# Three-step preparation of w_in's chunks, another order of the first loads, and 768 columns as two halves of 384

## Chip, cores and metric

The kernel runs on one core of one Trainium2 chip. The metric is the device time of one execution in microseconds; the kernel before takes 1076.66 us (median of three runs, 1076.47 to 1077.52).

## What is computed

Sigmoid attention over 4 batches of 12 heads (448 tokens, head width 64), then a gated block with a spatial mixing, then a residual two-layer block. The reference, cut:

```python
scores = scale * q @ k.T - log(S);  attn = sigmoid(scores);  x = attn @ v      # x: 4 x 448 x 768
h = relu(x @ w_in); u, v = h[..., :512], h[..., 512:]                          # w_in: 768 x 1024
v_n = (v - mean(v)) / sqrt(var(v) + 1e-6)
v_s = einsum('ts,bsd->btd', w_spatial, v_n) + b_spatial
x = (u * v_s) @ w_out                                                          # 512 x 768
xn = (x - mean(x)) / sqrt(var(x) + 1e-6) * g_ln
out = x + relu(xn @ w_ch1) @ w_ch2                                             # 768 x 3072 x 768
```

## The kernel before

**Products.** Every float32 operand of the large products is kept as a high and a low part; `mm3` (lines 252 to 255) issues three TensorE products for one: high x high, high x low, low x high. The instructions run in the order in which the code issues them; nothing reorders them. Each engine works through its own queue in order, and SyncE issues nearly all DMAs in order.

**w_in.** Its eight chunks of 768 columns (four of `wv_chunks`, then four of `wu_chunks`) arrive as raw 64-bit numbers. `w_load` (line 262) fetches one into one of two raw buffers. `w_decode` (267 to 283) makes a float32 of it: a scale on GpSimd for these chunks (line 273; ScalarE, line 275, for the chunks of the other weights), then three bit operations on VectorE (276, 277, 280). `split` (285) copies the high part on ScalarE (286) and subtracts on VectorE (287). `weight_jobs` (306) lines the steps up as load i, decode i-1, split i-2, and `jobs.pop` takes them from that line; the list `EARLY` says how many at each `beside()`. The first load stands ahead of the loop (line 775), before the first v load and the q and k loads of pair 2.

**Attention.** The loop of line 796 takes two head pairs an iteration, 12 iterations in all. An iteration issues: `rests` (line 415 products, one sigmoid, line 429 products, `x_end` of the pair before last), scores of two blocks (line 402), `sums` (line 442) and `x_end` of the last pair, the q and k loads of later pairs and `beside`, two more blocks, `sums`, `qk_split` of the next pairs (VectorE casts 381 and 384, GpSimd subtractions 385 and 386), two more blocks, `qk_split`, and then `bg.run`, the filler: the products of `x @ w_in` for batches already finished (`hv` with 512 columns, `hu` with 448), up to 9.2 us of them by the code's own costs. `hv` goes on with a block of w_in when its chunks were split at least `LAG` steps ago; `hu` starts when all eight were. Scores and rests write the tile `ps` with two buffers, sums the tile `psa` with two buffers, which `x_end` (line 286 copy, line 287 subtraction) frees.

**Wide outputs.** 768 output columns are written into the two PSUM banks of one `ps2` tile as 512 and 256 columns (`SPLIT`, `wide`). That happens in `Project.step`, 14 tiles with 24 products each, and in `ch2` of the last block, 12 groups of 14 tiles with 12 products each (lines 699 to 709); line 695 adds a tile to the residual. The very last tile is made as two parts, each added and stored by itself.

Of the kernel before, what the change touches and what calls it, by code (L numbers as in the profile page):

```python
# [10 lines left out]
F32 = mybir.dt.float32  # L11
# [3 lines left out]
ALU = mybir.AluOpType  # L15
# [12 lines left out]
NT = B * S  # L28
NCH = NT // P
HALF = DM // 2  # L30
SPLIT = [(0, 512), (512, 256)]
NB2 = 2 * S // P
EPS = 1e-6

# [5 lines left out]

BG_US = 2.3

LAG = 2
WARM = 10


EARLY = [1, 0, 0, 2, 0, 2, 1, 2, 1, 2, 1, 2, 1, 2, 1, 2]
WO_FROM = 30

VN_DVE = [range(4), range(4), (1, 3), (1, 3)]  # L50
# [153 lines left out]
def sigmoid_attention_gmlp_mlp(ctx: ExitStack, tc, q, k, v, w_in, w_sp, w_out, g_ln, w1, w2, out):  # L204
# [37 lines left out]
    def ps1():  # L242
        singles.append(singles.pop(0))
        return singles[-1]()

    def ps2():
        return ps_s.tile([P, 2, 512], F32, tag="ps2", name="ps2")

    def wide():
        return ps2().rearrange("p a n -> p (a n)")[:, :DM]  # L250

    def mm3(ps, lh, ll, rh, rl, first, last):
        nc.tensor.matmul(ps, lh, rh, start=first, stop=False)  # L253
        nc.tensor.matmul(ps, lh, rl, start=False, stop=False)  # L254
        nc.tensor.matmul(ps, ll, rh, start=False, stop=last)  # L255
# [8 lines left out]
        nc.sync.dma_start(raw.rearrange("p n t -> p (n t)"), src.bitcast(U32))  # L264
        return raw

    def w_decode(raw, first):
        blk = dec_r.next()
        f, bits = blk.ap(WC), blk.bits(WC)
        low, high = raw[:, :, 0], raw[:, :, 1]  # L270

        if first:
            nc.gpsimd.tensor_scalar(f, high.bitcast(F32), 2.0**-112, None, op0=ALU.mult)  # L273
        else:
            nc.scalar.mul(f, high.bitcast(F32), 2.0**-112)
        nc.vector.tensor_scalar(bits, bits, 3, None, op0=ALU.logical_shift_left)
        nc.vector.scalar_tensor_tensor(  # L277
            bits, low, 29, bits, op0=ALU.logical_shift_right, op1=ALU.bitwise_or
        )
        nc.vector.scalar_tensor_tensor(  # L280
            bits, high, 0x80000000, bits, op0=ALU.bitwise_and, op1=ALU.bitwise_or
        )
        return f

    def split(hi, lo, x, eng=nc.vector):
        nc.scalar.copy(hi, x)  # L286
# [2 lines left out]
    class Chunk:  # L289


        def __init__(self, src, place, first=False):
            self.src, self.place, self.ready, self.first = src, place, None, first

        def load(self):
            self.raw = w_load(self.src)

        def decode(self):
            self.f = w_decode(self.raw, self.first)

        def split(self):
            self.hi, self.lo = self.place()
            split(self.hi, self.lo, self.f)
            self.ready = now[0]

    def weight_jobs(chunks):
        n = len(chunks)
        for i in range(n + 2):
            if i < n:
                yield chunks[i].load  # L310
            if 1 <= i <= n:
                yield chunks[i - 1].decode
            if i > 1:
                yield chunks[i - 2].split

    def row_chunks(src, n, parts, first=False):
        def place(i):
            return lambda: [t.ap(n, WC)[:, i] for t in parts]

        return [Chunk(src[:, i * WC : (i + 1) * WC], place(i), first) for i in range(n)]  # L320

    jobs = Jobs()

# [273 lines left out]
    class Project:  # L597
# [6 lines left out]
        def step(self, c, g, xt, n, at):  # L604
            gh, gl = halves(g, n)
            wh, wl = (t.ap(NDC, DM) for t in self.wo)
            cols = slice(at, at + P)
            y = self.ys[c].ap(DM)
            ps = wide()
            for o, m in SPLIT:  # L610
                ws = slice(o, o + m)
                for d in range(NDC):
                    mm3(ps[:, ws], gh[:, d, cols], gl[:, d, cols], wh[:, d, ws], wl[:, d, ws], d == 0, d == NDC - 1)
            nc.scalar.copy(y, ps)
            self.norm()
# [44 lines left out]
    def mlp(xt, ys, wa, wb, first, hid_r, proj):  # L660
# [21 lines left out]
        def ch2(u, w, last):  # L682
            hh, hl = hid[u]
            u0, n = UNITS[u]
            for c in range(n // P):
                cols = slice(c * P, (c + 1) * P)
                row = u0 + c * P
                y = ys[row // P].ap(DM)
# [5 lines left out]
                def add(ps, ws):  # L694
                    nc.vector.tensor_add(y[:, ws], ps, y[:, ws])  # L695
                    if last:
                        nc.sync.dma_start(out[row : row + P, ws], y[:, ws])

                if last and row + P == NT:

                    for o, m in SPLIT:
                        ps, ws = ps1()[:, :m], slice(o, o + m)
                        part(ps, ws)
                        add(ps, ws)
                    continue
                ps = wide()
                for o, m in SPLIT:
                    part(ps[:, o : o + m], slice(o, o + m))
                add(ps, slice(0, DM))

        pend = None
        for g in range(NGRP):
# [39 lines left out]
        ch2(*pend)  # L752


    wv_chunks, wu_chunks = row_chunks(w_in[0], 4, wv, True), row_chunks(w_in[1], 4, wu, True)
    jobs.add(weight_jobs(wv_chunks + wu_chunks))
    wo = []
    wo_chunks = row_chunks(w_out, 4, wo)
    gated = []
# [12 lines left out]
    qk_load(1)  # L772
    qk_split(0)
    qk_split(1)
    jobs.pop(1)
    pv_load(0)
    qk_load(2)
    pv_load(1)
    step = iter(range(10**9))

    def beside():
        i = now[0] = next(step)
        jobs.pop(EARLY[i] if i < len(EARLY) else 2)
# [12 lines left out]
    for p in range(0, n_pairs, 2):  # L796
        if p:
            rests(p)
        scores((p, 0), (p, 1))
        if p:  # L800
            sums(p - 1)
            x_end(p - 1)
        else:
            rests(p)
        qk_load(p + 3)
        beside()
        qk_load(p + 4)
        pv_load(p + 2)
        pv_load(p + 3)
        if p + 2 == n_pairs:  # L810
            rq.free()
            rk.free()
            wsp_raw = F.alloc(5 * S)
            nc.sync.dma_start(wsp_raw.ap(5 * S), w_sp)
        scores((p, 2), (p + 1, 0))
        beside()
        sums(p)
        qk_split(p + 2)
        beside()
        scores((p + 1, 1), (p + 1, 2))  # L820
        qk_split(p + 3)
        beside()
        bg.run(4 * BG_US)
    rests(n_pairs)
    now[0] += 1
    sums(n_pairs - 1)
# [163 lines left out]
```

## Time and profile before

| | |
|---|---|
| median of the runs | 1076.66 us |
| the profiled execution's own time | 1080.43 us |
| its span in the trace | 1078.3 us |
| TensorE busy, products | 1063.5 us (99%) |
| VectorE, ScalarE, GpSimd busy | 545.1, 298.4, 114.7 us |
| mean granted TensorE clock | 0.994 |

The span runs from the first to the last instruction of the trace; the execution's own time has a little around it. Products are pipelined and the profile models their ends, so how densely TensorE works is read from the distance between the starts of its products. In the timeline a row has the start, the time from the first start to the last end, engine, line and operation, the tile written and read, the shapes, how many instructions are merged, and in brackets the idle time before with the instruction or DMA that ended it.

### The profile page before, as it was taken

To read this page: it belongs to the slowest core of one execution; us is meant where nothing else is said; L and a number is where in the kernel's file an instruction comes from. 1 tells how busy PE (TensorE), PEld (TensorE's weight loads), DVE (VectorE), ACT (ScalarE), POOL (GpSimd) and SP (SyncE) were. 2 spreads that over 40 slices of the span, in tenths; PEclk is the share of its full clock that TensorE was granted. 3 is DMA by queue.
4 is the path that set the end of the run, shared out by engine and by line. 5 is a ranking of instruction groups with operands and counts; after the bars stand their busy time and mean duration, and the time that the engine had idled before them with its cause. 6 is when DMAs were issued, how large, how long until landed. Compare 5 with 4: busy or idle time off the path is not lost.

```text
span 1078.3 us, 13999 instructions
## 1 busy us (share of the span) xinstructions
PE 1063.5 (99%) x5812; PEld 868.5 (81%) x5812; DVE 545.1 (51%) x789; ACT 298.4 (28%) x445; POOL 114.7 (11%) x104
## 2 busy tenths in 40 slices
PE   8889999999999999999999999999999999999998
PEld 4456666668989888888888888888888888888887
DVE  2663113207756856464645555564636464655533
ACT  4554445445623422121212121211212120212110
POOL 3452212202214410000000000000000000000000
PEclk8999999999999999999999999999999999999999
DMA  6743235325600112020111111020202021111013
GB/s 183 225 153 106 90 113 175 121 88 191 217 4 30 40 49 89 30 88 30 59 59 59 60 59 59 31 79 9 88 30 88 30 67 51 59 59 59 1 59 146
DMA packets 31951, 87.15 MB, mean 81 GB/s; under 512 B 7568, under 2 KB 15888, under 8 KB 31760
## 3 DMA queue, kind: packets, MB, share of 16 engines
q1 hardware_dynamic: 29808, 78.23, 22.2%
q0 software_dynamic: 1600, 7.34, 2.0%
q8 instruction: 46, 0.75, 0.3%
q10 hardware_dynamic: 480, 0.69, 0.2%
q14 instruction: 17, 0.14, 0.0%
HBM read 73.38 MB, written 12.86 MB: 80 GB/s over the span
## 4 chain that ended last, share of the span: by engine, by line
PE 94%; DVE 1%; POOL 1%; issue 1%; DMA 0%; ACT 0%; POOLq 0%; ACTq 0%; SPq 0%
PE ps L253 22%; PE ps L254 21%; PE ps L255 21%; PE psa L255 6%; PE psa L254 6%; PE psa L253 6%; PE psa L442 5%; PE ps L402 3%; POOL f_all L273 1%; PE ps L415 1%; PE psa L429 1%; PE ps L640 0%; PE psa L640 0%; DMA f_all<-in_w_in 0%; DVE f_all L277 0%
## 5 line engine op out<-in xcount | busy, mean ns | idle before, releaser
L253 PE MATMUL ps<-r_all 128*128 128x512 f32 (+2 forms) x1250 | 438.6, 351 | 0.0
L254 PE MATMUL ps<-r_all 128*128 128x512 f32 (+2 forms) x1250 | 436.9, 350 | 0.0
L255 PE MATMUL ps<-r_all 128*128 128x512 f32 (+2 forms) x1250 | 435.1, 348 | 0.0
L253 PEld LDWEIGHTS ps<-r_all 128*128 128x128 f32 x1250 | 236.6, 189 | 34.4 <-issue 4.1
L255 PEld LDWEIGHTS ps<-r_all 128*128 128x128 f32 x1250 | 235.9, 189 | 29.8
L254 PEld LDWEIGHTS ps<-r_all 128*128 128x128 f32 x1250 | 236.7, 189 | 28.4
L695 DVE TENSOR_TENSOR f_all<-ps,f_all 128x768 f32<-128x768 f32 x168 | 160.7, 956 | 164.4 <-PE ps L255 164.4
L253 PE MATMUL psa<-r_all 128*128 128x512 f32 (+2 forms) x338 | 122.9, 364 | 0.0
L255 PE MATMUL psa<-r_all 128*128 128x512 f32 (+2 forms) x338 | 122.8, 363 | 0.0
L254 PE MATMUL psa<-r_all 128*128 128x512 f32 (+2 forms) x338 | 122.8, 363 | 0.0
L677 ACT ACTIVATE r_all<-ps 128x512 fp32r<-128x512 f32 (+1 forms) x48 | 25.9, 540 | 275.6 <-PE ps L255 275.6
L286 ACT CAST r_all<-f_all 128x768 fp32r<-128x768 f32 x60 | 49.9, 834 | 170.4 <-DVE f_all L280 135.0
L389 ACT ACTIVATE f_all<-ps,bias_s 128x896 f32<-128x896 f32 x84 | 80.9, 1006 | 57.1 <-PE ps L402 32.0
L678 DVE SCALAR_TENSOR_TENSOR r_all<-psa,r_all 128x512 fp32r<-128x512 f32 (+1 forms) x48 | 29.9, 622 | 90.4 <-ACT r_all L677 90.4
L255 PEld LDWEIGHTS psa<-r_all 128*128 128x128 f32 x338 | 63.8, 189 | 9.4
L254 PEld LDWEIGHTS psa<-r_all 128*128 128x128 f32 x338 | 63.8, 189 | 9.4
L253 PEld LDWEIGHTS psa<-r_all 128*128 128x128 f32 x338 | 63.8, 189 | 9.4
L442 PE MATMUL psa<-f_all 128*64 128x448 f32 x288 | 63.4, 578 | 4.4 <-DVE r_all L287 4.4
L287 DVE TENSOR_TENSOR r_all<-psa,r_all 128x448 fp32r<-128x448 f32 (+1 forms) x38 | 22.3, 594 | 86.8 <-ACT r_all L286 86.8
L287 DVE TENSOR_TENSOR r_all<-f_all,r_all 128x768 fp32r<-128x768 f32 x60 | 57.1, 952 | 16.2 <-ACT r_all L286 16.1
L402 PEld LDWEIGHTS ps<-r_all 64*128 64x128 f32 x432 | 38.3, 188 | 32.2 <-issue 21.4
L277 DVE SCALAR_TENSOR_TENSOR f_all<-f_all 128x768 uint32<-128x768 uint32 x60 | 58.4, 973 | 2.1
(85 smaller groups left out, 672.2 us busy)
## 6 DMA issues: line engine op xcount, KB each, us to landing
f_all<-in_w SPq DMA_DIRECT2D x48, 768.0 KB, 4.2
f_all<-in_w_in SPq DMA_DIRECT2D x8, 768.0 KB, 5.3
f_all<-in_v SPq DMA_DIRECT2D x24, 256.0 KB, 3.6
f_all<-in_k SPq DMA_DIRECT2D x45, 112.0 KB, 2.8
f_all<-in_q SPq DMA_DIRECT2D x45, 112.0 KB, 2.9
out_y<-f_all SPq DMA_DIRECT2D x13, 384.0 KB, 2.3
vscr<-f_all SPq DMA_DIRECT2D x14, 256.0 KB, 2.0
uscr<-f_all SPq DMA_DIRECT2D x16, 224.0 KB, 1.9
```

Source lines behind the costliest of these rows:

```text
L253: nc.tensor.matmul(ps, lh, rh, start=first, stop=False)
L254: nc.tensor.matmul(ps, lh, rl, start=False, stop=False)
L255: nc.tensor.matmul(ps, ll, rh, start=False, stop=last)
L277: nc.vector.scalar_tensor_tensor(bits, low, 29, bits, op0=ALU.logical_shift_right, op1=ALU.bitwise_or)
L286: nc.scalar.copy(hi, x)
L287: eng.tensor_sub(lo, x, hi)
L389: nc.scalar.activation(af, ps[:, :, :S], AF.Sigmoid, bias=bias_s, scale=1.0 / math.sqrt(D))
L402: nc.tensor.matmul(ps[:, j, :S], a[w][rows, kc], a[x][rows], start=(i == 0), stop=(i == 2))
L442: nc.tensor.matmul(a["ps"][rows, :S], a["v"][:, 4 * j + c], af[:, j], start=(p % 2 == 0 and c == 0), stop=(p % 2 == 1 and c == 2),)
L677: nc.scalar.activation(hh[:, f], ps[:, :n], AF.Relu)
L678: nc.vector.scalar_tensor_tensor(hl[:, f], ps[:, :n], 0.0, hh[:, f], op0=ALU.max, op1=ALU.subtract)
L695: nc.vector.tensor_add(y[:, ws], ps, y[:, ws])
```

## The change

Scale, bit operations and split of a w_in chunk become three steps of their own, and a table, `W_IN_PLAN`, names for each iteration of the attention loop three places (A, behind the first scores; B, behind the first `qk_split`; C, behind the filler) and the steps issued there. The scale of the eight w_in chunks stays on GpSimd. The first w_in load moves behind the q and k loads of pair 2, the second behind those of pair 3, the others into the plan. `LAG` goes from 2 to 1. The wide outputs are written as two halves of 384 columns, one in each bank, and read by the copy, the add and the store as (2, 384).

```diff
-SPLIT = [(0, 512), (512, 256)]
-LAG = 2
+LAG = 1
-EARLY = [1, 0, 0, 2, 0, 2, 1, 2, 1, 2, 1, 2, 1, 2, 1, 2]
+W_IN_PLAN = {
+    "0B": ["scale 0"],
+    "1A": ["bits 0", "scale 1"],
+    "1B": ["split 0", "bits 1", "load 2"],
+    "2A": ["split 1", "load 3", "scale 2"],
+    "2B": ["bits 2", "scale 3"],
+    "3A": ["split 2", "bits 3", "load 4"],
+    "3B": ["split 3", "load 5", "scale 4"],
+    "3C": ["bits 4", "scale 5"],
+    "4A": ["split 4", "bits 5", "load 6"],
+    "4B": ["split 5", "load 7", "scale 6"],
+    "4C": ["bits 6", "scale 7"],
+    "5A": ["split 6", "bits 7"],
+    "5B": ["split 7"],
+}
     def wide():
-        return ps2().rearrange("p a n -> p (a n)")[:, :DM]
+        return ps2()[:, :, :HALF]
-    def w_decode(raw, first):
+    def w_scale(raw, pool):
         blk = dec_r.next()
+        f, high = blk.ap(WC), raw[:, :, 1].bitcast(F32)
+        if pool:
+            nc.gpsimd.tensor_scalar(f, high, 2.0**-112, None, op0=ALU.mult)
+        else:
+            nc.scalar.mul(f, high, 2.0**-112)
+        return blk
+
+    def w_bits(raw, blk):
+        bits = blk.bits(WC)
 ...
         def decode(self):
-            self.f = w_decode(self.raw, self.first)
+            self.scale(False)
+            self.bits()
 ...
-            for o, m in SPLIT:
-                ws = slice(o, o + m)
+            for h in range(2):
+                ws = slice(h * HALF, (h + 1) * HALF)
                 for d in range(NDC):
-                    mm3(ps[:, ws], gh[:, d, cols], gl[:, d, cols], wh[:, d, ws], wl[:, d, ws], d == 0, d == NDC - 1)
-            nc.scalar.copy(y, ps)
+                    mm3(ps[:, h], gh[:, d, cols], gl[:, d, cols], wh[:, d, ws], wl[:, d, ws], d == 0, d == NDC - 1)
+            nc.scalar.copy(self.ys[c].ap(2, HALF), ps)
 ...
                 ps = wide()
-                for o, m in SPLIT:
-                    part(ps[:, o : o + m], slice(o, o + m))
-                add(ps, slice(0, DM))
+                for h in range(2):
+                    part(ps[:, h], slice(h * HALF, (h + 1) * HALF))
+                add(ps, slice(0, 2))
 ...
+    def w_in_step(name):
+        for job in W_IN_PLAN.get(name, ()):
+            what, c = job.split()
+            getattr((wv_chunks + wu_chunks)[int(c)], what)()
 ...
     qk_split(0)
     qk_split(1)
-    jobs.pop(1)
     pv_load(0)
     qk_load(2)
+    wv_chunks[0].load()
     pv_load(1)
 ...
-        jobs.pop(EARLY[i] if i < len(EARLY) else 2)
+        jobs.pop(2)
 ...
         scores((p, 0), (p, 1))
+        w_in_step(f"{p // 2}A")
 ...
         qk_load(p + 3)
+        if not p:
+            wv_chunks[1].load()
         beside()
 ...
         qk_split(p + 2)
+        w_in_step(f"{p // 2}B")
         beside()
 ...
         bg.run(4 * BG_US)
+        w_in_step(f"{p // 2}C")
```

## Rows read from the trace of the kernel before

**Rows 1.** Timeline of TensorE, groups of products in the attention loop, 0 to 140 us

```profile
6.04 1.99 PE L402 MATMUL ps<-r_all 64*128 64x448 f32 x12 [0.95 <-DVE r_all L384]
8.52 1.16 PE L415 MATMUL ps<-f_all 64*64 64x448 f32 x6 [0.50 <-ACT f_all L389]
11.78 1.75 PE L415 MATMUL ps<-f_all 64*64 64x448 f32 x2 [2.09 <-DMA f_all<-in_q]
...
21.24 1.29 PE L415 MATMUL ps<-f_all 64*64 64x448 f32 x8 [0.49 <-DMA f_all<-in_q]
...
29.49 2.48 PE L442 MATMUL psa<-f_all 128*64 128x448 f32 x12 [0.96 <-DVE r_all L287]
...
34.20 1.97 PE L415 MATMUL ps<-f_all 64*64 64x448 f32 x7
...
44.49 4.17 PE L442 MATMUL psa<-f_all 128*64 128x448 f32 x12 [1.94 <-DVE r_all L287]
...
52.29 0.98 PE L415 MATMUL ps<-f_all 64*64 64x448 f32 x8
...
74.29 0.98 PE L415 MATMUL ps<-f_all 64*64 64x448 f32 x8
...
78.58 1.01 PE L402 MATMUL ps<-r_all 64*128 64x448 f32 x6 [1.76 <-ACT f_all L389]
...
99.22 0.98 PE L415 MATMUL ps<-f_all 64*64 64x448 f32 x8
...
117.25 0.98 PE L415 MATMUL ps<-f_all 64*64 64x448 f32 x8
...
138.42 0.98 PE L415 MATMUL ps<-f_all 64*64 64x448 f32 x8
```

**Rows 2.** Table by stretches, 40 to 60 us: engines' busy us, granted clock, DMA, GB/s

```profile
40.00:60.00 20.00, 17.32 (x105) 8.28 (x99) 13.91 (x18) 11.03 (x15) 9.28 (x7) 0.91 0.62 173
```

**Rows 3.** Lines of VectorE 20 to 80 us; SyncE's waits before 25; w_in's load (landing)

```profile
L276 DVE TENSOR_SCALAR f_all<-f_all 128x768 uint32<-128x768 uint32 x7 | 4.7, 666 | 19.1 <-POOL f_all L273 19.1
L287 DVE TENSOR_TENSOR r_all<-f_all,r_all 128x768 fp32r<-128x768 f32 x6 | 5.7, 950 | 0.0
...
SPq L264 <- DVE f_all L280: 10.1, 1, 10.1
...
DMA to landing us min/median/max: 4.5/5.3/8.4
```

**Rows 4.** Timeline of TensorE, starts of products of 512, 448 and 256 columns

```profile
68.08 0.39 PE L253 MATMUL ps<-r_all 128*128 128x512 f32 x1
...
70.12 0.39 PE L253 MATMUL ps<-r_all 128*128 128x512 f32 x1
...
90.00 0.36 PE L253 MATMUL ps<-r_all 128*128 128x448 f32 x1
...
92.03 0.36 PE L254 MATMUL ps<-r_all 128*128 128x448 f32 x1
...
702.17 0.40 PE L253 MATMUL ps<-r_all 128*128 128x512 f32 x1
...
703.55 0.28 PE L253 MATMUL ps<-r_all 128*128 128x256 f32 x1
...
704.27 0.40 PE L253 MATMUL ps<-r_all 128*128 128x512 f32 x1
```

**Rows 5.** Timeline of VectorE and GpSimd beside each other, 23 to 53 us

```profile
23.39 4.42 POOL L273 TENSOR_SCALAR f_all<-f_all 128x768 f32<-128x768 f32 x2
...
26.95 0.96 DVE L277 SCALAR_TENSOR_TENSOR f_all<-f_all 128x768 uint32<-128x768 uint32 x1
...
49.82 0.38 DVE L384 CAST r_all<-f_all 128x448 fp32r<-128x448 f32 x1
...
51.21 1.35 DVE L384 CAST r_all<-f_all 128x448 fp32r<-128x448 f32 x1
```

**Rows 6.** Costliest groups of the page, the add on VectorE

```profile
L695 DVE TENSOR_TENSOR f_all<-ps,f_all 128x768 f32<-128x768 f32 x168 | 160.7, 956 | 164.4 <-PE ps L255 164.4
```

More of the change, by code (lines that the diff above doesn't have):

```diff
@@ L265, in w_load @@
         return raw
-    def w_decode(raw, first):
+    def w_scale(raw, pool):
         blk = dec_r.next()
-        f, bits = blk.ap(WC), blk.bits(WC)
+        f, high = blk.ap(WC), raw[:, :, 1].bitcast(F32)
[6 more added lines that the diff above has]
+        bits = blk.bits(WC)
         low, high = raw[:, :, 0], raw[:, :, 1]
[L272 to L275, printed above, removed]
         nc.vector.tensor_scalar(bits, bits, 3, None, op0=ALU.logical_shift_left)
@@ L282, in w_decode @@
         )
-        return f
+        return blk.ap(WC)
     def split(hi, lo, x, eng=nc.vector):
@@ L289, in sigmoid_attention_gmlp_mlp, with __init__, scale, bits @@
     class Chunk:
-        def __init__(self, src, place, first=False):
-            self.src, self.place, self.ready, self.first = src, place, None, first
+        def __init__(self, src, place):
+            self.src, self.place, self.ready = src, place, None
         def load(self):
             self.raw = w_load(self.src)
+        def scale(self, pool=True):
+            self.blk = w_scale(self.raw, pool)
+        def bits(self):
+            self.f = w_bits(self.raw, self.blk)
         def decode(self):
-            self.f = w_decode(self.raw, self.first)
+            self.scale(False)
+            self.bits()
         def split(self):
@@ L304, in split, with row_chunks @@
             self.ready = now[0]
[L306 to L316, printed above, removed]
+    def row_chunks(src, n, parts):
         def place(i):
             return lambda: [t.ap(n, WC)[:, i] for t in parts]
-        return [Chunk(src[:, i * WC : (i + 1) * WC], place(i), first) for i in range(n)]
+        return [Chunk(src[:, i * WC : (i + 1) * WC], place(i)) for i in range(n)]
     jobs = Jobs()
@@ L687, in ch2 @@
                 row = u0 + c * P
-                y = ys[row // P].ap(DM)
+                y = ys[row // P].ap(2, HALF)
                 def part(ps, ws):
@@ L692, in part, with add @@
                         mm3(ps, hh[:, f, cols], hl[:, f, cols], w[1][f].hi[:, ws], w[1][f].lo[:, ws], f == 0, f == GF - 1)
-                def add(ps, ws):
-                    nc.vector.tensor_add(y[:, ws], ps, y[:, ws])
+                def add(ps, hs):
+                    nc.vector.tensor_add(y[:, hs], ps, y[:, hs])
                     if last:
-                        nc.sync.dma_start(out[row : row + P, ws], y[:, ws])
+                        nc.sync.dma_start(out[row : row + P].rearrange("p (h n) -> p h n", h=2)[:, hs], y[:, hs])
                 if last and row + P == NT:
-                    for o, m in SPLIT:
-                        ps, ws = ps1()[:, :m], slice(o, o + m)
-                        part(ps, ws)
-                        add(ps, ws)
+                    for h in range(2):
+                        ps = ps1()[:, :HALF]
+                        part(ps, slice(h * HALF, (h + 1) * HALF))
+                        add(ps.rearrange("p (h n) -> p h n", h=1), slice(h, h + 1))
                     continue
                 ps = wide()
-                for o, m in SPLIT:
-                    part(ps[:, o : o + m], slice(o, o + m))
-                add(ps, slice(0, DM))
+                for h in range(2):
+                    part(ps[:, h], slice(h * HALF, (h + 1) * HALF))
+                add(ps, slice(0, 2))
         pend = None
@@ L752, in mlp @@
         ch2(*pend)
-    wv_chunks, wu_chunks = row_chunks(w_in[0], 4, wv, True), row_chunks(w_in[1], 4, wu, True)
-    jobs.add(weight_jobs(wv_chunks + wu_chunks))
+    wv_chunks, wu_chunks = row_chunks(w_in[0], 4, wv), row_chunks(w_in[1], 4, wu)
+    def w_in_step(name):
+        for job in W_IN_PLAN.get(name, ()):
+            what, c = job.split()
+            getattr((wv_chunks + wu_chunks)[int(c)], what)()
     wo = []
```

## Prediction

> **What bounds the kernel now.** I read the timeline of TensorE first, by the start times of its products, because the busy share counts pipelined ends and shows no loss. From about 100 us on the products follow each other without a hole, and only fewer or denser products could help there. Before 100 us that isn't so. The attention loop has 12 iterations of two head pairs, and each begins with eight products of line 415. Those start at 21.24, 34.20, 52.29, 74.29, 99.22, 117.25 and 138.42 us [rows 1]. The iteration from 117.25 to 138.42 has no hole: 21.17 us, of which 45 filler products (lines 253 to 255, 512 columns) take 45 x 0.2267 = 10.2 (68.08 to 70.12 is nine of them [rows 4]). **A clean iteration is therefore 10.95 us plus filler.** Iteration 0, from 6.04, lacks one group of line 442 (2.48 with its pipelined end) and eight products like those of line 415 (0.98); start to start that is some 3.2 us, so its products would fill 7.75.
>
> What the early iterations lose against that: iteration 0 takes 15.20 us, lost 7.45. Iteration 1 (3 filler products) takes 12.96 against 11.63, lost 1.3. Iteration 2 (9 of them) 18.09 against 12.99, lost 5.1. Iteration 3 (42) 22.00 against 20.47, lost 1.5. Iteration 4 (51 of 448 columns at 0.203 [rows 4]) 24.93 against 21.30, lost 3.6. **In all 18.95 us of a span of 1078.3.** The releasers say why [rows 1]: the last line 415 products at 11.78 waited 2.09 for q; line 442 waited 0.96 at 29.49 and 1.94 at 44.49 for VectorE's line 287, which frees a PSUM accumulator; line 402 waited 1.76 at 78.58. VectorE was late because line 276 of each w_in chunk waits for GpSimd's scale, 19.1 us between 20 and 80 us [rows 3], with line 287 queued behind it. SyncE was blocked too: the third w_in load waited 10.1 us for a raw buffer [rows 3], the k and q loads of pairs 5 and 6 stood behind it, and line 415 of iteration 2, started at 34.20, took 1.97 us for seven products where eight take 0.98. Holes also cost clock: twelve products of line 442 take 2.48 us at 2.4 GHz, but 4.17 at 44.49, right behind the 1.94 hole, where the granted clock of the 20 us around it is 0.91 [rows 1, 2], so part of them ran at the 1.2 GHz level.
>
> **The change, part by part.** *Scale, bits and split apart.* The number of operations and their durations stay: GpSimd 2.2 us per chunk (4.42 for two), VectorE three bit operations of 0.67 to 0.96, some 2.6 us, and a 0.95 subtraction, ScalarE one copy [rows 3, 5]. Scale c now stands one place ahead of bits c, with about half an iteration (5 us) between them, so VectorE no longer stands still for the 2.2 us and its queue stays short. Behind the moved scale on GpSimd are the subtractions of the next head pair, two of some 1.1 us; their products come half an iteration later, so 2.2 us more are covered by about 2 to 4 us of slack. Without that cover each scale would cost its 2.2.
>
> *Loads.* w_in's first load goes behind the k and q of pair 2, so the 2.09 us for q at 11.78 should go: those bytes no longer share the DMA engines with 768 KB. What is late next is the PSUM pair `ps`: it has two buffers, each held by a sigmoid, and the 0.50 at 8.52 is such a wait [rows 1]. With three or four of them I place the start of iteration 1 at 15.6 instead of 21.24, that is, 1.8 of the 7.45 us stay. The load of chunk 2 moves behind the k, q and v loads of iteration 1 and behind bits 0, so SyncE no longer blocks for 10 us. Each later load has its buffer freed one place before it and half an iteration to land; landing took 4.5 to 8.4 us, median 5.3 [rows 3], so a late one can hold GpSimd's scale for 1 to 3 us, which the same slack covers at least in part.
>
> *Order of the filler.* By the plan, chunk 0 is ready at step 5, 1 at 7, 2 at 11, 3 at 13, the last at 21 (before: 17). Iterations 1 to 3 then have 3, 6 and 45 filler products, the same 54 as before; iteration 4 has none (before 51), because `hu` asks for all eight chunks. Its 10.35 us are done later in places where TensorE is the bound, so they cost nothing in themselves, but iteration 4 has no cover against a late VectorE. `LAG` 1 instead of 2 lets nothing through earlier: every chunk is at least two steps old where it is asked for. I cost it at nothing.
>
> *Sum for the stage.* 18.95 - 1.8 = 17.1 us can come back at most. I leave 3 us for new small waits in iterations 1 to 4 (one hole of the size of 0.96 or 1.76 in two of them [rows 1]): **-14 us, bounds -9 to -17.**
>
> *Two halves of 384.* The wide outputs have 168 + 14 tiles; 168 x 12 + 14 x 24 = 2352 products change their columns, and their number stays. From start to start a 512-column product takes 0.2267 us in a long run of its own, a 256-column one 0.120 (703.55 to 704.27 for six); the slope is 0.4167 ns a column with 13.3 ns on top [rows 4]. The change of width costs extra: the six 512-column products at 702.17 take 1.38 us instead of 1.36. A tile is 2.10 us; twelve on the line at 384 columns (0.1733) are 2.08. Tiles that come right behind 256-column products are 132 (in each of 12 groups three in each of three units, two in the last); over them that is 2.6 us, and the first products of the first layer behind such tiles save perhaps another 0.4: **-3.0 us.** No row has 384 columns. The bounds: at 448 columns the row gives 0.203, 3.0 ns above the line; with that excess it would be 2352 x 3.0 ns = 7.1 us more, so +4.1; below, -3.4 if all width effects go. I take the line, because 256 and 512 on either side both lie on it.
>
> The add on VectorE (line 695, 768 columns 0.96 us) [rows 6] reads the same 768 numbers in two banks and isn't the bound. At the very end the last part has 384 columns instead of 256: 128/768 x 0.96 = 0.16 us more, and a larger last store, so **+0.2 us.**
>
> Sum: -14 - 3.0 + 0.2 = -16.8. The profiled execution took 1080.43 us with a span of 1078.3; that makes 1063.6. The median of the runs is 3.77 below the profiled execution, and I let that stand: **1059.9 us.**
>
> **A rule against the change.** Beside GpSimd's subtraction a cast on VectorE takes 1.35 us instead of 0.38; but line 277, which reads two SBUF operands, ran in 0.96 us at 26.95 right beside a scale (23.39 to 27.81) [rows 5]. The Trainium skill, "SBUF — State Buffer", section "Who interferes with whom", says that VectorE and GpSimd share a port pair held for a whole instruction, by copies and casts in the two-port mode and also by a VectorE instruction with two SBUF inputs against a GpSimd one that reads SBUF. The cast rows agree with it, the row of line 277 doesn't. By the rule, setting scale and bits side by side gains nothing; that is rival C.
>
> **Rivals.**
> B, the clock still falls. If holes of 1.5 to 2 us stay in iterations 0 and 2 or 4, the stretch behind each runs at 1.2 GHz as at 44.49; two such events cost some 3 us each (a hole of 1.8 and 1.5 more for a line 442 group). For it: iteration 4 has lost its filler. Against: the plan takes away the releasers of these holes. The stage then gives -8: 1065.9.
> C, engines take turns. Four scales (1, 2, 3 and 6) lie in iterations without much filler; if VectorE stands still during each, 4 x 2.2 = 8.8 us stay: -5.2 for the stage, 1068.7.
> E, 384 columns carry the excess of 448: +7.1 on the forecast, 1067.0.
> N, the change doesn't do what it says: the first scales and bits only move the hole to another instruction of the same queues, and the halves give nothing: 1076.5. Against it: with two chunks in an iteration VectorE has four casts (1.5 us), bits (5.2) and three subtractions of under 1 us [rows 3, 5], some 9 us in an iteration of 11.
> D, slower: the halves start 1536 bytes into the row, where neither 512 nor 256 columns ever began, and each product pays for it. At 0.185 us it is 2352 x 10 ns = 23.5 us on today's 0.175, minus 14: 1086. It decides from 0.181 on; the ceiling is 0.203, a longer product's time [rows 4]. Against: the line.
>
> **How the numbers follow.** Forecast 0.52 (own range 1056 to 1064), B 0.20, C 0.12, E 0.06, N 0.04, D 0.06. Faster by over 0.2% (2.2 us, about what measurements here can tell apart): 0.52 + 0.20 + 0.12 + 0.06 = 0.90; within it 0.04; slower 0.06. The range takes the forecast with both bounds, B, E and most of C: 1055.5 to 1068.7.
>
> **What would show it.** Right: the line 415 groups start near 15.6, 27, 39, 60 and 71 us, no line 442 or 402 product waits over 1 us, the idle time of line 276 behind the scale is near nothing, the load of line 264 no longer blocks SyncE for 10 us, and wide tiles take 2.08 us. B: a clock under 1.00 after 20 us. C: line 277 or 280 well above 0.96 us. D and E: starts of the 384-column products 0.176 us apart or more. Wrong altogether: holes of the same sum at other lines before 90 us, or a stage end later than today's minus 9 us.

## The result and the profile after

The median fell from 1076.57 us (4 runs, 1074.61 to 1077.52) to **1065.54 us** (4 runs, 1064.85 to 1066.03): ratio 0.9899, 95% interval 0.9882 to 0.9917, so 11.0 us or 1.0% faster. The forecast was 1059.9 us in a range of 1055.5 to 1068.7. The profiled execution of the changed kernel took 1065.46 us with a span of 1063.3; that of before took 1080.43 with 1078.3. Between these two executions the difference is 15.0 us, four more than between the medians. That gap is the first thing to explain.

The page of after: span, busy times, TensorE and its granted clock in 40 slices, the chain of waits, and the wide add that answers [rows 6].

```profile
span 1063.3 us, 14008 instructions
PE 1055.5 (99%) x5812; PEld 914.0 (86%) x5812; DVE 550.7 (52%) x789; ACT 298.2 (28%) x445; POOL 118.1 (11%) x104
PE   8999999999999999999999999999999999999998
PEclk9999999999999999999999999999999999999999
PE 96%; DMA 1%; DVE 1%; issue 0%; POOL 0%; ACT 0%; ACTq 0%; DVEq 0%; SPq 0%
...
L709 DVE TENSOR_TENSOR f_all<-ps,f_all 128x768 f32<-128x768 f32 x168 | 160.4, 955 | 163.1 <-PE ps L268 163.1
```

The timeline of TensorE after, attention loop (answers [rows 1]; line 402 of before is 416 now, 415 is 429, 442 is 456, 287 is 304):

```profile
5.92 1.99 PE L416 MATMUL ps<-r_all 64*128 64x448 f32 x12 [0.30 <-DVE r_all L398]
8.41 1.32 PE L429 MATMUL ps<-f_all 64*64 64x448 f32 x8 [0.50 <-ACT f_all L403]
...
16.01 2.18 PE L429 MATMUL ps<-f_all 64*64 64x448 f32 x7 [0.49 <-DMA f_all<-in_k]
...
29.22 1.02 PE L429 MATMUL ps<-f_all 64*64 64x448 f32 x8
...
41.56 0.98 PE L429 MATMUL ps<-f_all 64*64 64x448 f32 x8
...
62.71 0.98 PE L429 MATMUL ps<-f_all 64*64 64x448 f32 x8
...
74.00 1.16 PE L429 MATMUL ps<-f_all 64*64 64x448 f32 x8 [0.49 <-ACT f_all L403]
...
82.21 2.65 PE L456 MATMUL psa<-f_all 128*64 128x448 f32 x12 [1.05 <-DVE r_all L304]
...
96.73 0.98 PE L429 MATMUL ps<-f_all 64*64 64x448 f32 x8
```

The holes of 2.09, 0.96, 1.94 and 1.76 us are gone, and so is one of 1.45 at 60.71, also behind line 287, that the prediction did not list. One hole over 1 us is left, 1.05 at 82.21, and the granted clock stays at 1.00 behind it: the twelve products there take 2.65 us, where before's at 44.49 took 4.17. The table by stretches shows the granted clock (the number before the DMA share; [rows 2] had 0.91 in the second stretch):

```profile
0.00:20.00 20.00, 17.30 (x100) 10.41 (x102) 5.61 (x15) 10.12 (x12) 6.52 (x9) 1.00 0.85 231
...
40.00:60.00 20.00, 20.00 (x118) 12.63 (x117) 12.74 (x17) 11.90 (x15) 12.66 (x9) 1.00 0.55 166
```

Lines of VectorE from 20 to 80 us (busy, mean ns | idle before and its releaser), and SyncE's waits before 97 us (sum, times, longest); they answer [rows 3]:

```profile
L294 DVE SCALAR_TENSOR_TENSOR f_all<-f_all 128x768 uint32<-128x768 uint32 x7 | 8.9, 1275 | 0.2
L304 DVE TENSOR_TENSOR r_all<-f_all,r_all 128x768 fp32r<-128x768 f32 x6 | 7.4, 1239 | 6.6 <-ACT r_all L303 6.6
...
L293 DVE TENSOR_SCALAR f_all<-f_all 128x768 uint32<-128x768 uint32 x7 | 5.4, 778 | 1.1 <-POOL f_all L284 1.1
```

```profile
SPq L277 <- DVE f_all L297: 10.8, 4, 3.3
```

VectorE stood 19.1 us behind GpSimd's scale, and now 1.1. SyncE's w_in loads wait 3.3 us at most for bit operations, not 10.1, and 10.8 us in all up to 97 us, where before's waited 21.3. The median landing of these loads is 5.2 us (5.3 before).

What each iteration loses against the clean 10.95 us plus its filler, by the prediction's own measure (starts of the rest groups; filler of after 3, 6, 45, 0 and 51 products in iterations 1 to 5):

| kernel | start of it. 1 | it. 1 | it. 2 | it. 3 | it. 4 | it. 5 |
|---|---|---|---|---|---|---|
| before | 21.24 | 1.33 | 5.09 | 1.54 | 3.62 | 0.10 |
| after | 16.01 | 1.57 | 0.03 | 0.00 | 0.34 | 1.43 |

By the end of iteration 5 both have done as much filler if before is given a clean filler-free iteration more: 99.22 + 10.95 = 110.17 against 96.73, so **13.4 us** come from the attention stage. Later marks agree. The last transposes of the block's end and the last product of the kernel, timeline of before:

```profile
388.10 0.49 PE L640 MATMUL ps<-warm,f_all 128*128 128x128 f32 x3
...
1074.47 0.28 PE L255 MATMUL psa<-r_all 128*128 128x256 f32 x1
```

and of after:

```profile
374.20 0.49 PE L654 MATMUL psa<-warm,f_all 128*128 128x128 f32 x3
...
1059.40 0.34 PE L268 MATMUL ps<-r_all 128*128 128x384 f32 x1
```

That is 13.90 us earlier at the transposes and 15.07 at the last product, so the wide outputs behind them give 1.17; 0.1 goes back at the tail (span end minus the last start: 3.83 before, 3.93 after).

### The profile page after: what moved, and what is told of

Its sections match the earlier page's. It is cut to its first block, busy times and chain, and to the rows that moved or that the text cites. A ratio compares the mean times of both kernels' runs of the same rounds, so it can differ in the third digit from the quotient of the medians.

```text
span 1063.3 us, 14008 instructions
## 1 busy us (share of the span) xinstructions
PE 1055.5 (99%) x5812; PEld 914.0 (86%) x5812; DVE 550.7 (52%) x789; ACT 298.2 (28%) x445; POOL 118.1 (11%) x104
## 4 chain that ended last, share of the span: by engine, by line
PE 96%; DMA 1%; DVE 1%; issue 0%; POOL 0%; ACT 0%; ACTq 0%; DVEq 0%; SPq 0%
PE ps L266 22%; PE ps L268 22%; PE ps L267 22%; PE psa L268 6%; PE psa L267 6%; PE psa L266 6%; PE psa L456 5%; PE ps L416 4%; PE ps L429 1%; PE psa L443 1%; DMA f_all<-in_k 1%; PE psa L654 0%; PE ps L654 0%; DMA f_all<-in_w_in 0%; DMA f_all<-in_q 0%; DVE f_all L294 0%
## 5 line engine op out<-in xcount | busy, mean ns | idle before, releaser
L266 PE MATMUL ps<-r_all 128*128 128x384 f32 (+2 forms) x1250 | 435.8, 349 | 0.0
L268 PE MATMUL ps<-r_all 128*128 128x384 f32 (+2 forms) x1250 | 433.8, 347 | 0.0
L267 PE MATMUL ps<-r_all 128*128 128x384 f32 (+2 forms) x1250 | 433.6, 347 | 0.0
L268 PE MATMUL psa<-r_all 128*128 128x512 f32 (+3 forms) x338 | 123.6, 366 | 0.0
L267 PE MATMUL psa<-r_all 128*128 128x512 f32 (+3 forms) x338 | 123.4, 365 | 0.0
L266 PE MATMUL psa<-r_all 128*128 128x512 f32 (+3 forms) x338 | 123.0, 364 | 0.0
L691 ACT ACTIVATE r_all<-psa 128x512 fp32r<-128x512 f32 (+1 forms) x48 | 26.0, 541 | 276.5 <-PE psa L268 276.5
L692 DVE SCALAR_TENSOR_TENSOR r_all<-ps,r_all 128x512 fp32r<-128x512 f32 (+1 forms) x48 | 29.9, 623 | 90.6 <-ACT r_all L691 90.6
L304 DVE TENSOR_TENSOR r_all<-f_all,r_all 128x768 fp32r<-128x768 f32 x60 | 59.6, 994 | 23.6 <-ACT r_all L303 23.6
L294 DVE SCALAR_TENSOR_TENSOR f_all<-f_all 128x768 uint32<-128x768 uint32 x60 | 60.6, 1009 | 2.1
L456 PE MATMUL psa<-f_all 128*64 128x448 f32 x288 | 59.6, 548 | 1.1 <-DVE r_all L304 1.1
```

What stands on the lines that cost most here:

```text
L294: nc.vector.scalar_tensor_tensor(bits, low, 29, bits, op0=ALU.logical_shift_right, op1=ALU.bitwise_or)
L304: eng.tensor_sub(lo, x, hi)
L456: nc.tensor.matmul(a["ps"][rows, :S], a["v"][:, 4 * j + c], af[:, j], start=(p % 2 == 0 and c == 0), stop=(p % 2 == 1 and c == 2),)
L691: nc.scalar.activation(hh[:, f], ps[:, :n], AF.Relu)
L692: nc.vector.scalar_tensor_tensor(hl[:, f], ps[:, :n], 0.0, hh[:, f], op0=ALU.max, op1=ALU.subtract)
```

## Experiments

My theory was that of the prediction: the separated scale frees VectorE, the moved first load frees q, the unblocked SyncE frees k and q, and 384 columns lie on the line. The first rival: one of these parts carries nearly all of it. The second, formed from the results: it is neither the distance of scale from bits nor a load, but the place of the bit operations in VectorE's queue relative to the subtraction that frees the PSUM accumulator. Every ratio is to the kernel before on the same chip (medians 1075.32 to 1075.43 there).

### Halves alone

```diff
 (before)
-SPLIT = [(0, 512), (512, 256)]
+            for h in range(2):
+                ws = slice(h * HALF, (h + 1) * HALF)
...
```

> The kernel before with the wide outputs as two halves of 384 and nothing else. Theory of the prediction (a product costs 0.4167 ns a column plus 13.3 ns, and only 512-column products behind 256-column ones pay extra): 3.0 us less than before, about 1073.6. Rival, read from the trace of the changed kernel: every run of products behind one of another width pays some 30 to 40 ns, also behind 384 columns, so the price moves to the first layer's products: 1.0 to 1.5 us less, about 1075.3, and the 384-column products stand 0.1733 us apart.

Measured: 1074.40 us, ratio 0.9992 (0.9982 to 1.0001). So 0.9 us, hardly more than nothing, and no loss: the line holds, D and E fall, but so does the size. The starts of after show where it went: 384 columns in a long run, and the products of 512 columns that stand behind such a run.

```profile
482.48 0.33 PE L266 MATMUL ps<-r_all 128*128 128x384 f32 x1
...
486.67 0.39 PE L266 MATMUL psa<-r_all 128*128 128x512 f32 x1
...
490.79 0.39 PE L266 MATMUL ps<-r_all 128*128 128x512 f32 x1
...
689.77 0.33 PE L268 MATMUL ps<-r_all 128*128 128x384 f32 x1
...
693.93 0.33 PE L268 MATMUL ps<-r_all 128*128 128x384 f32 x1
```

From 689.77 to 693.93 lie 24 products: 4.16 / 24 = 0.1733, the forecast cadence to the last digit. But eighteen products of 512 columns right behind 384 take 4.12 (486.67 to 490.79) where 18 x 0.2267 = 4.08, and 24 of 384 right behind 512 take 4.19 (482.48 to 486.67) where the run takes 4.16. Over all such places of the last stage that is 34 times 0.040 and 35 times 0.027, 2.3 us. In before, a 512 run behind 256 columns cost 0.027 more, and a 256 run behind 512 gained 0.008; both stand there 167 times, 3.3 us in all. The change of width is not gone; it moved from inside the tile to the boundary with the first layer.

The same profile says something of before. Up to iteration 1 its attention loop has the order of before, yet:

```profile
8.32 2.16 PE L414 MATMUL ps<-f_all 64*64 64x448 f32 x8 [0.50 <-ACT f_all L388]
...
16.76 1.29 PE L414 MATMUL ps<-f_all 64*64 64x448 f32 x8 [0.49 <-ACT f_all L388]
...
40.02 4.17 PE L441 MATMUL psa<-f_all 128*64 128x448 f32 x12 [2.00 <-DVE r_all L286]
```

From 8.32 to 16.76 are 8.44 us where before's profile had 12.72 (8.52 to 21.24 [rows 1]), with no wait for q. The other losses are before's: 1.36, 5.09, 1.51 and 3.60. So the 2.09 wait and the slow stretch behind it came in the execution that was profiled, and do not come in every execution of this order; how often they come is not shown. By the sum that gave 13.4 us (its iteration 5 starts at 94.71, so 94.71 + 10.95 against 96.73) the change is worth 8.9 us of the stage against this profile.

### The plan without the halves

```diff
 (after)
+SPLIT = [(0, 512), (512, 256)]
-        return ps2()[:, :, :HALF]
+        return ps2().rearrange("p a n -> p (a n)")[:, :DM]
...
```

> The changed kernel with its wide outputs back at 512 and 256 columns. If the two parts of the change add up, this one is slower than the changed kernel by what the halves are worth: 1.0 to 1.5 us by the rival (about 1066.8), 3.0 by the prediction (about 1068.5). Its attention stage should end, for equal filler, 13.4 us earlier than in the profile of before.

Measured: 1067.23 us, ratio 0.9927 (0.9914 to 0.9939). Iterations lose 1.41, 0.01, 0.00, 0.34 and 1.66, as in after. From the last transposes to the last product it takes 686.15 us, as before's 388.32 to 1074.47; the two kernels with halves (after, and halves alone) take 684.98. So the halves are worth 1.2 us where they are used. Between runs the figure is looser: 0.9 alone, and in the plan 1.7 and 2.5 by the medians of after's two runs, 3.0 and 3.8 by the ratios. Alone, the parts give 0.9 and 8.1 us, 9.0 of the 10.7 to 11.0; the rest lies within the intervals, so the runs neither show nor exclude that the two help each other.

### After, once more

The changed kernel itself on the chip of the later runs.

> The changed kernel itself, beside the three others on one chip and for a second profile. Its profile should repeat: iteration starts near 16, 29.2, 41.6, 62.7 and 74 us within 0.5 us, no clock below full between 6 and 1060 us, and a profile within 1 us of the median of the runs, where the profile of before lay 3.8 above it. If the starts differ by over 2 us from execution to execution, the differences of 2 us between the other runs' profiles mean nothing.

Measured: 1064.78 us, ratio 0.9892 (0.9876 to 0.9909), the profiled execution 0.3 from the median; losses 0.52, 0.03, 0.00, 0.33 and 2.20. After's time hardly varies between executions, and its profile stands for it. The starts do not repeat within the 0.5 us that was expected: iterations 2 to 4 begin 1.0 us earlier than in the first profile (28.22, 40.56 and 61.72). Small losses in iterations 1 and 5 trade against each other from one execution to the next, by about 1 us, so a difference of that size between two single profiles tells nothing.

### The first load moved, alone and taken back

```diff
 (before)
-    jobs.pop(1)
     pv_load(0)
     qk_load(2)
+    jobs.pop(1)
```

> The kernel before with w_in's first load behind the q and k loads of pair 2, and nothing else. Theory of the loads (the front of the stage is lost to the transfer and to the clock that falls behind the wait for q): iteration 0 shrinks from 15.2 to about 10 us, the second group of line 415 products starts near 16, and the time falls by some 5 us, to 1071.5. Theory of the queues (VectorE's wait for the scale stays, and the scale now comes later): iteration 0 shrinks too, but iterations 1 and 2 lose part of it again: 2 to 4 us less, 1073 to 1074.5.

Measured: 1075.40 us, ratio 1.0004 (0.9995 to 1.0012): nothing, where both theories expected a gain. Iteration 1 starts at 15.64, as forecast, but iterations 1 to 4 then lose 3.25, 3.38, 6.02 and 0.15, 12.8 us together where before lost 11.6. The queue behind is as late as ever, and one hole grows:

```profile
25.80 2.48 PE L442 MATMUL psa<-f_all 128*64 128x448 f32 x12 [1.44 <-DVE r_all L287]
...
40.77 2.48 PE L442 MATMUL psa<-f_all 128*64 128x448 f32 x12 [1.66 <-DVE r_all L287]
...
57.08 4.75 PE L442 MATMUL psa<-f_all 128*64 128x448 f32 x12 [3.23 <-DVE r_all L287]
```

Inside the plan the other way round:

```diff
 (after)
+    wv_chunks[0].load()
     pv_load(0)
     qk_load(2)
-    wv_chunks[0].load()
```

> The changed kernel with w_in's first load back in front of the first v load and the loads of pair 2. The prediction gave the order of the first loads 5.6 us; the run with that move alone gave none, because scale and bits stayed one step in the queues behind. If the plan lets the gain through: 3 to 5 us slower than the changed kernel, with iteration 0 at 8.4 or at 12.7 us. Rival (the first loads aren't worth anything in either order, the wait of 2.1 us for q was one execution's): within 1 us of the changed kernel.

Measured: 1066.04 us, ratio 0.9913 (0.9895 to 0.9931), 1.3 us over the run of after beside it by medians and 2.3 by ratios, with overlapping intervals, and less than the 3 to 5 expected. Iteration 1 starts at 17.69 instead of 16.07. The move is worth 1 to 2 us at most, and only in the plan did it show any gain.

### The third load

```diff
 (before)
-EARLY = [1, 0, 0, 2, 0, 2, 1,
+EARLY = [1, 0, 0, 1, 0, 3, 1,
```

> The kernel before with w_in's third load (chunk 2) taken from the job line two places later, at step 5 behind the k, q and v loads of iteration 1, and nothing else. Theory of the blocked SyncE (the load that waits for its raw buffer holds back the loads of pairs 5 and 6): the wait of 10 us of the load on VectorE goes, the line 415 products of iteration 2 find their q, and iteration 2 loses 1.3 to 3 us less, so 1 to 3 us below before. Rival (the queues of VectorE and GpSimd hold the products back whatever the loads do): within 1 us of before, and the hole in front of line 442 in iteration 2 grows by what the loads give. The stretch up to iteration 1 is as in the kernel before; whether it takes 12.7 or 8.4 us from the first line 415 product tells whether the wait for q and the fallen clock there belong to the code or to one execution.

Measured: 1075.55 us, ratio 1.0005 (0.9993 to 1.0017). The load of chunk 2 no longer waits (the longest wait of a w_in load is now 5.2 us, that of chunk 4), and by itself that brings nothing: losses 1.33, 5.91, 0.76, 1.97 and 0.10, 9.97 in iterations 1 to 4 against before's 11.58 in its profiled execution. Here too the first rest group to iteration 1 takes 8.55 us, not 12.72.

```diff
 (after)
+    "0C": ["load 2"],
-    "1B": ["split 0", "bits 1", "load 2"],
+    "1B": ["split 0", "bits 1"],
```

> The changed kernel with the load of chunk 2 at the end of iteration 0, ahead of the q, k and v loads of iteration 1, where SyncE must wait for bits 0. Theory of the blocked SyncE: those loads come some 5 to 8 us later, the products of line 429 in iteration 2 and the casts of pair 5 wait, and the stage loses 2 to 5 us: 1066.5 to 1069.5 if the changed kernel stands at 1064.5 on this chip. Rival: within 1 us of the changed kernel.

Issued ahead of bits 0, load 2 fills the buffer that bits 0 reads; in this kernel the bit operations of chunk 0 read chunk 2's numbers. Measured: 1070.94 us, ratio 0.9952 (0.994 to 0.9965). SyncE did not block at this load, so it tests something else than I meant: VectorE waited for the transfer, with everything queued behind it, and iteration 1 lost 5.72 us.

```profile
27.58 0.96 DVE L295 SCALAR_TENSOR_TENSOR f_all<-f_all 128x768 uint32<-128x768 uint32 x1 [5.77 <-DMA f_all<-in_w_in]
...
30.45 0.49 PE L267 MATMUL ps<-r_all 128*128 128x512 f32 x1 [2.04 <-ACT r_all L304]
```

What it would cost to have SyncE blocked at load 2 in the changed kernel stays open; the eighth run, below, shows it for load 6.

### Scale next to its bits, and bits ahead of the subtraction

```diff
 (after)
-    "0B": ["scale 0"],
-    "1A": ["bits 0", "scale 1"],
-    "1B": ["split 0", "bits 1", "load 2"],
+    "1A": ["scale 0", "bits 0"],
+    "1B": ["split 0", "scale 1", "bits 1", "load 2"],
...
```

> The changed kernel with each scale moved from one place ahead directly in front of its bit operations; loads, splits and halves stay. Theory of the queues (what helps is that VectorE no longer stands still for the 2.2 us of a scale): the holes in front of line 456 return in iterations 1, 2, 4 and 5, the stage loses 4 to 9 us: 1069.5 to 1074.5. Rival (the order of the loads is the gain and the scale's place isn't): within 1 us of the changed kernel, 1065 to 1066.5.

Measured: 1067.03 us, ratio 0.9922 (0.991 to 0.9934). VectorE waits for four of the eight scales again, 13.2 us in the first 100 us (1.3 in after, 19.1 in before), and the loss is small: 1.06, 1.01, 0.07, 0.34 and 4.34 in iterations 1 to 5, against the two runs of after 1.5 and 2.3 us by medians, 2.5 and 3.2 by ratios, 3.1 between the spans. The profiled execution is the slowest of its five (1068.44 us, mean clock 0.998; the others have 1.000). Its one big hole, 2.44 us at 83.92, stands behind the bits that are issued at the end of an iteration without filler, ahead of line 303's subtraction:

```profile
80.25 0.56 DVE L292 TENSOR_SCALAR f_all<-f_all 128x768 uint32<-128x768 uint32 x1 [4.26 <-POOL f_all L283]
...
83.25 0.61 DVE L303 TENSOR_TENSOR r_all<-psa,r_all 128x448 fp32r<-128x448 f32 x1
```

**The step on which the forecast rested, scale apart from bits, carries between a seventh and a third of the gain.**

Then, from that kernel, two chunks are set one place earlier, to the end of the iteration before, where VectorE's queue reaches them ahead of the subtraction that frees the accumulator:

```diff
 (the kernel above)
-    "1A": ["scale 0", "bits 0"],
+    "0C": ["scale 0", "bits 0"],
...
-    "3A": ["split 2", "scale 3", "bits 3", "load 4"],
+    "2C": ["scale 3", "bits 3"],
+    "3A": ["split 2", "load 4"],
```

> The kernel with scale and bits together (the fourth run), with scale 0 and bits 0 moved from place A of iteration 1 to the end of iteration 0, and scale 3 and bits 3 from A of iteration 3 to the end of iteration 2: in front of line 303's subtraction that frees the PSUM accumulator, where the kernel before had them. Theory of the place: VectorE then waits for the scale with that subtraction behind it, holes of 1 to 2 us come back in front of line 455 in iterations 1 and 3, 2 to 5 us more than the fourth run. Rival (the place doesn't matter, only the number of chunks per iteration): within 1 us of the fourth run.

Measured: 1073.05 us, ratio 0.9972 (0.9961 to 0.9983): 6.0 us more than the kernel above by medians, 5.4 by ratios, for the same operations. Losses 2.32, 0.02, 6.12, 0.34 and 2.80. Nearly all of the difference is chunk 3, in iteration 3 (6.12 instead of 0.07); the hole expected in iteration 1 is 0.73 us, not 1 to 2, and what chunk 0 adds there (1.26) iteration 2 mostly gives back (0.99). VectorE, GpSimd and TensorE beside each other in iteration 3:

```profile
47.14 2.17 POOL L284 TENSOR_SCALAR f_all<-f_all 128x768 f32<-128x768 f32 x1
49.34 0.56 DVE L293 TENSOR_SCALAR f_all<-f_all 128x768 uint32<-128x768 uint32 x1 [4.13 <-POOL f_all L284]
...
51.81 0.62 DVE L304 TENSOR_TENSOR r_all<-psa,r_all 128x448 fp32r<-128x448 f32 x1
...
52.48 4.75 PE L456 MATMUL psa<-f_all 128*64 128x448 f32 x12 [3.41 <-DVE r_all L304]
```

VectorE stands 4.13 us for the scale (GpSimd's two subtractions run first, from 45.05 to 47.17), then does three bit operations (2.5 us), and only then, at 51.81, the subtraction for which TensorE has been waiting. With the bits behind it, in the kernel above, that subtraction starts at 44.42 without a wait for GpSimd, and the same group of products runs without a hole:

```profile
44.42 0.62 DVE L303 TENSOR_TENSOR r_all<-psa,r_all 128x448 fp32r<-128x448 f32 x1 [0.70 <-ACT r_all L302]
...
48.72 2.48 PE L455 MATMUL psa<-f_all 128*64 128x448 f32 x12
```

This was before's pattern too: 0.96 and 1.94 us at line 442 behind line 287 [rows 1]. The theory of place expected 2 to 5 us and got somewhat more, since the products behind the hole also ran at the lower clock (4.75 us for twelve instead of 2.48). One thing is not separated: with the place, VectorE's waits for the scale rose too, from 13.2 to 19.9 us. What the place costs with the scale apart, and so without these waits, was not run.

### Other engines and places

```diff
 (after)
-        def scale(self, pool=True):
+        def scale(self, pool=False):
```

> The changed kernel with the eight scales on ScalarE instead of GpSimd, at the same places. Theory of the turns (a scale or subtraction on GpSimd and an instruction on VectorE hold each other up: line 294 took 1.55 and 1.78 us beside GpSimd in the changed kernel, 0.96 alone): line 294 falls to 0.96 in more places, the losses of iterations 1 and 5 (1.6 and 1.4 us) shrink, the time falls by 0.5 to 1.5 us. Rival (ScalarE's sigmoids are nearer the path than GpSimd: a scale of 0.9 us in front of a sigmoid delays the scores): 1 to 3 us slower than the changed kernel.

Measured: 1071.37 us, ratio 0.9956 (0.9942 to 0.997). Iteration 1 loses 0.69 instead of 1.57, but after's second profile, with the scales on GpSimd, has 0.52 there, so no gain is shown. Line 294 still takes 1.76 us once, at 76.39, beside a subtraction of GpSimd. And iteration 5 loses 8.69:

```profile
80.60 0.89 ACT L286 ACTIVATE f_all<-f_all 128x768 f32<-128x768 f32 x1 [6.33 <-DMA f_all<-in_w_in]
...
82.44 1.49 PE L416 MATMUL ps<-r_all 64*128 64x448 f32 x6 [6.30 <-ACT f_all L403]
```

The last load lands at 80.5 us in this kernel as in after. On GpSimd, in after, the scale for it starts at 80.70 behind an idle time of 0.89 us, with nothing urgent queued behind it; ScalarE came to it early and stood 6.33 us, with the sigmoids that free `ps` queued behind.

Bits 4, load 6 and scale 5 ahead of iteration 3's filler, and the first two w_in loads later:

```diff
 (after)
-    "3C": ["bits 4", "scale 5"],
-    "4A": ["split 4", "bits 5", "load 6"],
+    "3P": ["bits 4", "load 6", "scale 5"],
+    "4A": ["split 4", "bits 5"],
...
+        w_in_step(f"{p // 2}P")
         bg.run(4 * BG_US)
```

> The changed kernel with two moves. The first: bits 4, load 6 and scale 5 stand in front of the filler of iteration 3 instead of behind it, so that they run under its 45 products and not behind line 525, which waits for them. The second: in iteration 0 w_in's first load goes behind the loads of pair 3 and its second behind those of pair 4, with scale 0 at the end of iteration 0. If the losses left in the changed kernel come from these two (iteration 1 waits for q until 18.04 us, iteration 5 for late bits 6): iterations 1 and 5 lose under 0.5 us each, 2 to 3 us less in all, about 1062. Rival (scale 0 and scale 1 come later and hold up bits 0 and 1, or other waits take their place): within 1 us of the changed kernel, 1064.5.

Measured: 1068.73 us, ratio 0.9938 (0.9925 to 0.9951). Iteration 5 loses less (0.78, where after's two profiles have 1.43 and 2.20), iteration 1 loses 0.50, as after's second profile, and iteration 4 loses 5.61: load 6 waited 10.5 us in SyncE's queue for bits 4, ahead of the filler's own stores, and ScalarE waited for these.

```profile
67.21 0.60 ACT L521 ACTIVATE f_all<-ps 128x512 f32<-128x512 f32 x1 [7.75 <-DMA vscr<-f_all]
...
68.76 1.29 PE L416 MATMUL ps<-r_all 64*128 64x448 f32 x6 [3.39 <-ACT f_all L403]
```

```diff
 (the kernel above)
-    "3P": ["bits 4", "load 6", "scale 5"],
-    "4A": ["split 4", "bits 5"],
+    "3P": ["bits 4", "scale 5"],
+    "4A": ["split 4", "bits 5", "load 6"],
```

> The eighth run with load 6 back behind the filler at place A of iteration 4. There it stood on SyncE in front of the stores of the filler and waited for bits 4; the stores held ScalarE's line 521 and through it the products, a hole of 3.4 us and a fallen clock in iteration 4. If that load was all, iteration 4 takes 11.3 us again, iterations 1 and 5 lose under 1 us, and the time is 1 to 2 us below the changed kernel. Rival (bits 4 in front of line 525 hold up the filler by themselves): a hole stays in iteration 3 or 4, same time as the changed kernel or slower.

Measured: 1065.02 us, ratio 0.9898 (0.988 to 0.9915). The hole in iteration 4 is gone (0.34), so load 6 alone had made it: SyncE blocked at that place cost 5.3 us of the stage. Iteration 5 loses 2.01. No version was faster than the change itself.

## Why the prediction was right, and where it was not

**Direction and range: right; the size of the stage in part by luck.** The stage was put at -14 and gave -13.4 between the profiled executions, but 4.2 us of that came from the one execution of before (below); against the profile of the halves alone it is 8.9. Iteration 1 was put at 15.6 and starts at 16.01; 3 us were left for new small waits in iterations 1 to 4, and these lose 1.94 together, iteration 5 another 1.43. The later starts were put at 27, 39, 60 and 71 and are 29.22, 41.56, 62.71 and 74.00: late by the 1.57 of iteration 1, the 0.4 of the start, and sums rounded down. Filler as planned, 3, 6, 45, none and 51; the iteration without cover lost 0.34. The tail was put at 0.2 and cost 0.1.

**The step that failed: "The median of the runs is 3.77 below the profiled execution, and I let that stand."** The sum was made against an execution with a 2.09 us wait for q and a fallen clock behind it, 12.72 us from the first rest group to iteration 1. Two other profiles with the same order there have 8.44 and 8.55, so some 4.2 us of the gain that the sum booked were gains over that one execution. Taking the offset off again counted them twice: after's profiled execution lies 0.1 below its median, before's 3.9 above. Without the offset the forecast is 1063.6, 1.9 below the 1065.54 measured.

**The term that was mis-sized: the halves, "-3.0 us".** In the last stage they gave 1.2. The cadence was exact, 0.1733; the step "the first products of the first layer behind such tiles save perhaps another 0.4" had the wrong sign. Behind 384 columns these products cost 0.040 a run more than in a steady run, behind 256 it had been 0.027, and the step back to 384 costs 0.027 where that to 256 gained 0.008.

**The attribution: half wrong.** "Scale c now stands one place ahead of bits c ... so VectorE no longer stands still" happened (19.1 to 1.1 us), but was not what most of the time hung on: with scale and bits together 1.5 to 3 us of the 11 are lost. The prediction saw the right pair, line 276 waiting with line 287 queued behind it, and credited the removed wait; the larger lever was the queue's order. Putting two chunks back ahead of the subtraction costs 5 to 6 us, nearly all of it by one of them, chunk 3. The shares by the runs, taken in this order, are therefore: scale apart 1.5 to 3 us, place of the bits 5 to 6, and the 3 that the kernel with both put back still gains (0.9972) to halves, first load and the rest of the plan. They are not shares in any order: the place was moved only with the scale next to its bits. "The load of chunk 2 ... SyncE no longer blocks" is worth nothing alone, and "the start of iteration 1 at 15.6 instead of 21.24" was worth 1 to 2 us at that place in the runs (17.69 to 16.07 in the plan, 16.76 to 15.64 without it), not 5.6.

**LAG at nothing, and the port rule.** `LAG` was not run apart; by the plan each chunk is at least two steps old where it is used, so its cost of nothing is argued and not measured. Rival C was half there. VectorE and GpSimd beside each other in after (answers [rows 5]):

```profile
20.61 2.63 POOL L284 TENSOR_SCALAR f_all<-f_all 128x768 f32<-128x768 f32 x1 [0.49 <-DMA f_all<-in_w_in]
...
21.20 1.55 DVE L294 SCALAR_TENSOR_TENSOR f_all<-f_all 128x768 uint32<-128x768 uint32 x1
...
73.30 1.85 POOL L400 TENSOR_TENSOR r_all<-f_all,r_all 128x448 fp32r<-128x448 f32 x1
...
78.35 1.46 POOL L400 TENSOR_TENSOR r_all<-f_all,r_all 128x448 fp32r<-128x448 f32 x1
...
78.85 1.78 DVE L294 SCALAR_TENSOR_TENSOR f_all<-f_all 128x768 uint32<-128x768 uint32 x1
80.66 0.96 DVE L297 SCALAR_TENSOR_TENSOR f_all<-f_all 128x768 uint32<-128x768 uint32 x1
80.70 2.97 POOL L284 TENSOR_SCALAR f_all<-f_all 128x768 f32<-128x768 f32 x1 [0.89 <-DMA f_all<-in_q]
```

Line 294 takes 1.55 and 1.78 us beside GpSimd, where alone it takes 0.96; a subtraction of GpSimd at 73.30, beside VectorE's own subtraction and cast, takes 1.85 where 1.1 is usual, and at 80.70 VectorE keeps its 0.96 and the scale takes 2.97 instead of 2.2. The two engines do get in each other's way, and often both pay: the scale at 20.61 takes 2.63, the subtraction at 78.35 takes 1.46. The Trainium skill, "SBUF — State Buffer", section "Who interferes with whom", names such a pair; the trace agrees that it interferes, and shows 0.6 to 0.8 us a time for line 294, not a whole operation in turn. So C's price of 2.2 us a scale did not arise, though its sign, a bit operation well above 0.96, did. Whether the contention is free is not shown: the subtraction that ends the 1.05 us hole at 82.21 starts at 81.54, right behind the slowed rows.

**The rivals.** The measured time lies where B was put (1065.9), but not for its reason: the clock is 1.00 through the whole kernel, and without the offset, which B's figure carries too, B stands at 1069.6. B's mechanism itself is real: behind holes of 1.76 to 6.30 us in the variants the granted clock fell, though not behind all of them. N, E and D fall with the ratio and the cadence.

## What to carry to other kernels

In an engine's in-order queue look first at what stands behind a long or waiting piece of work: moving the operation that another engine waits for ahead of it was worth more here (5 to 6 us) than then taking the waits that were left away (1.5 to 3 us), and it costs no instruction. A wait can sit where nothing urgent is queued behind it with little harm, and costs much on an engine that frees PSUM for TensorE: 6.33 us on ScalarE made a hole of 6.30, 4.13 on VectorE one of 3.41. And before an offset between a profiled execution and the median is carried over, ask whether the loss that makes the offset is the very one that the sum removes.

## What was not expected of the hardware

- A change of moving width between runs of products has its own price: 0.040 us behind 384 for 512 columns, 0.027 for 384 behind 512, 0.027 for 512 behind 256, -0.008 for 256 behind 512. The steady cadence at 384 columns is 0.1733, on the line of 256 and 512 (0.120 and 0.2267), while 448 had 0.203.
- Holes of about the same length did and did not lower the clock: behind 2.44 us (scale with its bits, 83.92) twelve products took 4.15 us, with a granted clock of 0.91 from 80 to 100 us; behind 2.40 (bits ahead, 90.23) they took 2.64, with 1.00. The rows here do not tell what decides between them.

```profile
83.92 4.15 PE L455 MATMUL psa<-f_all 128*64 128x448 f32 x12 [2.44 <-DVE r_all L303]
```

```profile
90.23 2.64 PE L456 MATMUL psa<-f_all 128*64 128x448 f32 x12 [2.40 <-DVE r_all L304]
```
